# Two token pairs of 480 columns instead of one of 448, a shorter weight conversion and a bank for each of the last tiles, in an attention and two feed-forward layers on one core

## The chip, the core and the metric

The kernel runs on one core of a Trainium2 chip. The metric is the device time in microseconds (us); the time before is the median of three runs. Engines: TensorE (PE) with its weight loads (PEld), VectorE (DVE), ScalarE (ACT), GpSimd (POOL, unused here) and SyncE (SP), which issues nearly all DMAs.

## What is computed

```
# q, k, v: 1 x 6016 x 256;  w_in: 256 x 2048;  w_out: 2048 x 256, twice (float64)
qn = q / (norm(q, over tokens) + 1e-6);  kn the same
a = softmax(kn^T @ qn / tau)             # 256 x 256, over channels
x = v @ a                                # 6016 x 256
x = relu(x @ w_in)**2 @ w_out            # layer 1
h = x @ w_in2
out = maximum(0.01 * h, h) @ w_out2      # layer 2
```

## The kernel before

Tokens are columns: everything after the attention works on transposed activations, and a matmul streams one half of a token pair. Six pairs (`WIDTH`, line 59) cover the 6016 tokens, each of two halves of `WIDTH[p]` columns; `FIRST` holds where each begins. The program goes through the pairs twice, once for layer 1 and once for layer 2. In a pass over a pair the 2048 hidden channels are eight groups of 256; one group is a unit (`unit`, line 1396).

Values are float32 split in a high part, rounded by a copy to fp32r, and a low part, the difference (`low`, line 115). Each product is three matmuls (`mm3`, line 560): low by high, high by high, high by low. A unit has first products (x by `w_in`) and second products (g by `w_out`). Where the code says form P, the second products are eight of three matmuls; in form S they are seven, by Strassen's scheme, with sums kept in bank c (`yA`) and bank e (`yF`). First products are seven in every pair but the first of layer 1. `GROUPS` (line 56) says which groups of which pairs have form S: six of eight in the last two pairs of layer 1, seven in layer 2, five in its last pair. A unit with Strassen's first products and form P has 45 matmuls (21 and 24).

The weights come as float64 in pairs of 32-bit words. A `Unit` (lines 130 to 215) loads 256 x 256 of them into `wst`, makes float32 of them on DVE and ACT, rounds and splits them and stores them to DRAM for the passes that follow: `exponent`, `mantissa`, `mantissa_low`, `sign`, `high` on DVE and `rebias`, `round` on ACT. `w0` and `w1` are the low and the high word. The 16 units of layer 2, all but one in blocks with Strassen sums (`sums`, line 217), go through one buffer, `wis` (bufs=1): the cast in `round` fills it, DVE adds the low part, and SP stores it. The sums of layer 1's `w_out` (`wo_sums`, line 1307) use the same buffer.

The first two units of layer 1's `w_in` are converted during the attention (`converted`, line 307), step by step between the tiles of q and k. The scores are summed over 47 tiles on PE (line 404), the norms by squares on ACT and sums on DVE; then come the softmax and the fold of it into `w_in`. The first weights of `w_out` (`first_o`) begin there too.

At the end, the second half of the last pair takes its last two groups by tokens (`second_by_tokens`, line 596): g is the stationary side, and four tiles of 128 tokens by 256 channels come out, two to a bank. `finish_last` (line 612) adds to each the sums kept so far (`last_sums`) and stores it.

The order is not that of the code. `build` lists tasks with engine, cost, due time and the tasks they wait for; `simulate` (line 826) runs them by due time, in several turns (`TURNS`), with `PIPE` taken off the costs; the best plan is then written out engine by engine. `place` gives each result tile one of two rings, c or wst. On each engine instructions then run strictly in that order. `seeded` (line 978) says where a unit's first sum is made on PE and ACT rather than on DVE.

Of the kernel before, what the change touches and what calls it, by code (L numbers as in the profile page):

```python
# [19 lines left out]
P = 128  # L20

REBIAS = -896.0 * 2**23
# [7 lines left out]
def attn_moe_moe2(  # L33
# [25 lines left out]
    WIDTH = [512, 512, 512, 512, 448, 512]  # L59
# [32 lines left out]
    rebias = const.tile([P, 1], F32, name="rebias")  # L92
    nc.vector.memset(rebias, REBIAS)
# [36 lines left out]
    class Unit:  # L130
# [16 lines left out]
        def exponent(self):  # L147
            self.e = cpool.tile([P, 2, 2 * P], U32, tag="ce", name="ce")
            ts(self.e, self.w1, 0x7FF00000, None, op0=ALU.bitwise_and)

        def rebias(self):
            nc.scalar.activation(self.e, self.e, AF.Relu, bias=rebias, scale=8.0)

        def mantissa(self):
            self.m = cpool.tile([P, 2, 2 * P], U32, tag="cm", name="cm")
            ts(self.m, self.w1, 0x000FFFFF, 0x00100000, op0=ALU.bitwise_and, op1=ALU.bitwise_or)

        def mantissa_low(self):
            stt(raw(self.m), self.w0, 2.0**-32, self.m, op0=ALU.mult, op1=ALU.add)

        def sign(self):
            stt(self.e, self.w1, 0x80000000, self.e, op0=ALU.bitwise_and, op1=ALU.bitwise_or)

        def high(self):
            m, e = raw(self.m), raw(self.e)
            if self.blocks:
                self.x = cpool.tile([P, 8, P], F32, tag="whl", name="wr")
                if self.kind == "i":
                    to = self.x[:, :4].rearrange("p (k b) m -> p k (b m)", b=2)
                else:  # L170
                    to = self.x[:, :4].rearrange("p (k b) (q c) -> k p (b q) c", b=2, c=B)
                    m, e = (y.rearrange("p b (q k c) -> k p (b q) c", q=Q, k=KC) for y in (m, e))
                    for k in range(KC):
                        stt(to[k], m[k], 2.0**-20, e[k], op0=ALU.mult, op1=ALU.mult)
                    return
                stt(to, m, 2.0**-20, e, op0=ALU.mult, op1=ALU.mult)
                return
            stt(m, m, 2.0**-20, e, op0=ALU.mult, op1=ALU.mult)
            self.x = m
# [127 lines left out]
    def converted(units):  # L307

        units[0].exponent()
        later[ACT].append(units[0].rebias)  # L310
        yield
        for i, u in enumerate(units):
            if i + 1 < len(units):
                units[i + 1].exponent()
                later[ACT].append(units[i + 1].rebias)
                yield
            for step in (u.mantissa, u.mantissa_low, u.sign, u.high):
# [13 lines left out]
    with (  # L331
# [40 lines left out]
        STEPS = {2: 3, 3: 2}  # L372
# [80 lines left out]
        run(steps[1], 3)  # L453
# [29 lines left out]
        first_o.exponent()  # L483
# [112 lines left out]
    def second_by_tokens(n, fb):  # L596


        L, p, g = units[n]
        wo, gt = wo_t[L, p, g], g_t[n, 1]  # L600
        for t in range(WIDTH[p] // P):
            for m, (a, b) in enumerate(((0, 1), (0, 0), (1, 0))):
                nc.tensor.matmul(
                    y_bank(L, p, 1, t // 2)[:, t % 2 * C : (t % 2 + 1) * C],
                    gt[:, a, fb, t * P : (t + 1) * P],
                    wo[:, b, :, fb],
                    start=(g, fb) == (BY_TOKENS, 0) and m == 0 and t % 2 == 0,
                    stop=m == 2,
                    skip_group_check=True,
                )  # L610

    def finish_last():

        p = NP - 1
        ys = [y_t[2, p, 1, d] for d in range(KC)]
        to = rows(out, p, 1).rearrange("(t p) c -> p t c", p=P)
        o = [vpool.tile([P, 2, C], F32, tag="v", name="o"), tpool.tile([P, 2, C], F32, tag="s", name="o")]
        for b, copy in enumerate((nc.vector.tensor_copy, nc.scalar.copy)):
            ob = o[b].rearrange("p t (q k c) -> p t q k c", q=Q, k=KC)
            y = ys[b].rearrange("p (t k q c) -> p t q k c", t=2, q=Q, k=KC)  # L620
            if last_sums:
                sums = last_sums["t"].rearrange("p t (q k c) -> p t q k c", q=Q, k=KC)
                for t in range(2):
                    add(ob[:, t], y[:, t], sums[:, 2 * b + t])
            else:
                copy(ob, y)
# [136 lines left out]
    PIPE = {"DVE": (0.09, 0.45), "ACT": (0.1, 0.5), "PE": (0, 0.5), "POOL": (0, 0.6)}  # L763
# [5 lines left out]

    class Buf:  # L770


        def __init__(self, tag, bufs, due):
            self.due, self.bufs, self.users, self.alloc, self.tag = due, bufs, [], None, tag
            lines.setdefault(tag, []).append(self)
# [23 lines left out]
    def place(free_lines, held):  # L799

        known = {t: sorted((b.due, b.due + 60) for b in lines.get(t, ())) for t in free_lines}
        for b in sorted(lines.pop("any", ()), key=lambda b: b.due):

            def free(t):
                before = [e for d, e in known[t] if d <= b.due]
                return sorted(before)[-3] if len(before) >= 3 else 0

            b.tag = min(free_lines, key=free)
            known[b.tag].append((b.due, b.due + b.held))
# [78 lines left out]
    WHOLE = True  # L888
    TAIL = 12
    TURNS = 12  # L890
    FIRST_MIXED = min([p for L, p in GROUPS if L == 1], default=0)
    CONV_BEGIN, CONV_END = 1.2, 4.3
# [74 lines left out]
    BATCHES = {4: (4,), 5: (3, 2), 6: (3, 3), 7: (4, 3)}  # L967
# [23 lines left out]
    def build(base):  # L991
        tasks.clear()
        c_tag.clear()
        lines.clear()
        fixed, firsts, items = [], [], []
# [23 lines left out]
        ce_b = {0: Buf("ce", 2, -10)}  # L1019
# [3 lines left out]
        def convert(u, due, loaded=None, first=None, pace=4, begin=0):  # L1023
# [10 lines left out]
            if u is first_o:  # L1034
                ce = ce_b[0]
                t = None
            else:
                ce = Buf("ce", 2, d(0))
                t = T("DVE", 1.9, d(0), u.exponent, deps=deps, alloc=ce, uses=[w])
            re = T("ACT", 3.2, d(0.5), u.rebias, deps=[t], uses=[ce])  # L1040
            cm = Buf("cm", 2, d(1))
            t = T("DVE", 1.9, d(1), u.mantissa, deps=deps, alloc=cm, uses=[w])
            ml = T("DVE", 3, d(2), u.mantissa_low, deps=[t], uses=[w, cm])
            t = T("DVE", 3, d(3), u.sign, deps=[re, ml], uses=[w, ce])
            if blocks:
                raw_ = Buf("whl", 2, d(4))
                t = T("DVE", 3, d(4), u.high, deps=[t], alloc=raw_, uses=[ce, cm])
# [6 lines left out]
            else:  # L1054
                t = T("DVE", 3, d(4), u.high, deps=[t], uses=[ce, cm])
# [496 lines left out]
        def plain_items(n, order=order8):  # L1552
            L, p, g = units[n]
            if (L, p) == (2, NP - 1) and g >= BY_TOKENS:
                out_ = [plain_item(n, *o) for o in order[:4]]
                for fb in range(2):
                    x = queue(n, 6.35, second_by_tokens, (n, fb),
                              [low_of[n, 1], wo_ready[L, p, g], *y_after.get((L, p, 1, 0), ()), *y_after.get((L, p, 1, 1), ())],
# [157 lines left out]
        def combine_last(L, p):  # L1716
# [14 lines left out]
            y_after[L, p, 0, 1], y_after[L, p, 0, 0], y_after[L, p, 1, 1], y_after[L, p, 1, 0] = [y11], [y21], [y12], [y22]  # L1731
            key = L, p, "sums"
# [49 lines left out]
        free = simulate(PE(fixed, list(firsts), items))  # L1782
# [65 lines left out]
```

## Time and profile before

| | us |
|---|---|
| median of three runs | 1004.73 |
| lowest, highest | 1003.47, 1004.86 |
| the profiled execution's own time | 1005.9 |
| its span, first to last instruction | 1004.1 |
| PE busy | 998.2 |
| DVE busy | 920.8 |
| ACT busy | 803.7 |

The span is what the profile sees; 1.8 us lie around it. PE busy means that a matmul was under way, and matmuls overlap: the start of the next one is what counts, so the price of one is read from a row of the chain that merges several. Rows give their start, their length and, in brackets, how long the engine was idle before and what released it.

### The profile page before, as it was taken

Reading aid. Unit: us, or ns where it says so; the run is one execution under the profiler, and the core shown is the slowest. Engines: PE = TensorE matmul, PEld = TensorE weight load, DVE = VectorE, ACT = ScalarE, POOL = GpSimd, SP = SyncE. Lnnn points to the kernel's source line nnn. Section 1 sums busy time; section 2 is a strip of 40 time slices with the busy share of each in tenths; the row PEclk is TensorE's granted clock in tenths of the full one; section 3 lists DMA queues with packets and bytes.
Section 4 is the critical chain, followed back from the end, with each engine's and each line's share of the span. In section 5 each row is a group of like instructions: output and inputs, shape, how many; then the busy total and the mean of one; then the engine's idle time right before and its main releaser. Section 6 shows DMA issues by size and latency. Waiting matters only on the chain.

```text
span 1004.1 us, 13173 instructions
## 1 busy us (share of the span) xinstructions
PE 998.2 (99%) x4540; PEld 840.8 (84%) x4540; DVE 920.8 (92%) x1371; ACT 803.7 (80%) x1181; POOL 0.7 (0%) x6
## 2 busy tenths in 40 slices
PE   9999999999999999999999999999999999999998
PEld 8888888888887888898888888888888888998887
DVE  5999989999999999999998999999999999999985
ACT  6788877887878787887888888878888888887773
POOL 0000000000000000000000000000000000000000
PEclk9999999999999999999999999999999999999999
DMA  9796469869988977966756656577576577576643
GB/s 353 286 227 213 168 207 261 282 224 328 309 274 275 359 268 287 312 209 201 235 179 233 218 198 223 182 211 257 166 223 229 176 235 230 208 232 220 206 130 85
DMA packets 162035, 233.93 MB, mean 233 GB/s; under 512 B 53296, under 2 KB 97328, under 8 KB 159664
## 3 DMA queue, kind: packets, MB, share of 16 engines
q1 hardware_dynamic: 161248, 232.43, 70.6%
q8 instruction: 36, 0.59, 0.2%
q10 hardware_dynamic: 720, 0.66, 0.2%
q14 instruction: 31, 0.25, 0.1%
HBM read 186.12 MB, written 46.92 MB: 232 GB/s over the span
## 4 chain that ended last, share of the span: by engine, by line
PE 95%; DMA 3%; ACT 1%; DVE 1%; SPq 0%; issue 0%; ACTq 0%; DVEq 0%
PE y L562 36%; PE ha L562 20%; PE hb L562 15%; PE yA L562 7%; PE h L724 4%; PE yF L562 3%; PE hc L562 3%; PE sT L404 3%; PE he L562 2%; PE pw L265 1%; DMA qk<-in_k_dram 1%; DMA wo<-wis 1%; DMA qk<-in_q_dram 1%; DMA out_dram<-o 0%; ACT c L701 0%; ACT wis L205 0%
## 5 line engine op out<-in xcount | busy, mean ns | idle before, releaser
L562 PE MATMUL y<-g,wo 128*128 128x512 f32 (+1 forms) x1344 | 350.5, 387 | 0.0
L562 PEld LDWEIGHTS y<-g,wo 128*128 128x128 f32 x1344 | 252.2, 188 | 49.1
L562 PE MATMUL ha<-x,wi 128*128 128x512 f32 (+1 forms) x912 | 252.6, 385 | 0.2 <-ACT u L1421 0.2
L116 DVE TENSOR_TENSOR g<-c,g 128x1024 fp32r<-128x1024 f32 (+1 forms) x192 | 228.1, 1196 | 12.0 <-ACT g L694 7.0
L562 PEld LDWEIGHTS ha<-x,wi 128*128 128x128 f32 x912 | 170.9, 188 | 33.1 <-ACT c L1421 0.8
L562 PE MATMUL hb<-x,wi 128*128 128x512 f32 (+1 forms) x684 | 189.3, 385 | 0.0
L562 PEld LDWEIGHTS hb<-x,wi 128*128 128x128 f32 x684 | 128.0, 188 | 24.5 <-DVE c L571 0.6
L1526 DVE TENSOR_TENSOR c<-c 128x512 f32<-128x512 f32 (+1 forms) x208 | 139.9, 673 | 7.4
L1501 ACT CAST g<-c 128x1024 fp32r<-128x1024 f32 (+1 forms) x104 | 104.9, 1023 | 3.4 <-DVE c L1526 1.2
L116 DVE TENSOR_TENSOR b<-c,b 128x512 fp32r<-128x512 f32 (+1 forms) x156 | 102.9, 668 | 1.7 <-ACT b L1519 1.6
L1519 ACT CAST b<-c 128x512 fp32r<-128x512 f32 (+1 forms) x156 | 93.0, 608 | 13.0 <-DVE c L1526 7.1
L701 ACT ACTIVATE c<-c 128x1024 f32<-128x1024 f32 (+1 forms) x96 | 100.2, 1044 | 1.5
L694 ACT CAST g<-c 128x1024 fp32r<-128x1024 f32 (+1 forms) x88 | 91.9, 1046 | 2.0 <-PE y L562 0.3
L1421 ACT COPY w<-ha 128x512 f32<-128x512 f32 (+1 forms) x76 | 43.8, 576 | 51.2 <-PE ha L562 50.8
L711 ACT ACTIVATE c<-c 128x512 f32<-128x512 f32 (+1 forms) x98 | 60.7, 621 | 7.7 <-DVE c L571 7.5
L1421 ACT COPY u<-ha 128x512 f32<-128x512 f32 (+1 forms) x76 | 43.7, 575 | 7.3 <-PE ha L562 5.3
L724 PE MATMUL h<-x,wi 128*128 128x512 f32 x192 | 47.9, 391 | 0.0
L116 DVE TENSOR_TENSOR x<-xr,x 128x1024 fp32r<-128x1024 f32 (+3 forms) x44 | 46.6, 1064 | 0.1
L562 PE MATMUL y<-b,ws 128*128 128x512 f32 (+1 forms) x156 | 43.0, 384 | 0.0
L562 PE MATMUL yA<-g,wo 128*128 128x512 f32 (+1 forms) x156 | 43.0, 384 | 0.0
L562 PE MATMUL y<-b,wo 128*128 128x512 f32 (+1 forms) x156 | 43.0, 384 | 0.0
L562 PE MATMUL yF<-g,ws 128*128 128x512 f32 (+1 forms) x156 | 43.0, 383 | 0.0
(133 smaller groups left out, 1269.9 us busy)
## 6 DMA issues: line engine op xcount, KB each, us to landing
wi<-wi SPq DMA_DIRECT2D x80, 896.0 KB, 5.7
wo<-wo SPq DMA_DIRECT2D x84, 512.0 KB, 4.7
ws<-wo SPq DMA_DIRECT2D x120, 128.0 KB, 3.4
wi<-wi SPq DMA_DIRECT2D x24, 512.0 KB, 5.0
wst<-in_moe_w_in_dram SPq DMA_DIRECT2D x16, 512.0 KB, 6.1
wst<-in_moe_w_out_dram SPq DMA_DIRECT2D x16, 512.0 KB, 5.8
wi<-wis SPq DMA_DIRECT2D x8, 896.0 KB, 4.9
wo<-wis SPq DMA_DIRECT2D x7, 1024.0 KB, 5.9
```

Of the source, the lines that this page charges most:

```text
L116: tt(lo, x, raw(hi), op=ALU.subtract)
L265: nc.tensor.matmul(pw[:, i * 2 * P : (i + 1) * 2 * P], eT[:, a, j, i * P : (i + 1) * P], whl[g][:, b, j], start=t == 0 and (i == 0 or g == 0),
L404: nc.tensor.matmul(sT[j][:, :C], t[:, 0, i, j * P : (j + 1) * P], t[:, 1, i], start=n == 0 and i == 0, stop=last_tile and i == g - 1,)
L562: nc.tensor.matmul(ps, a[m], b[n], start=first and i == 0, stop=i == 2, skip_group_check=True)
L694: nc.scalar.copy(g_t[n, half][:, 0, :, :w], c)
L701: nc.scalar.activation(c, c, AF.Square)
L711: nc.scalar.activation(c, c, AF.Prelu, alpha=0.01)
L724: nc.tensor.matmul(h_t[n, half, fb][:, :w], a[i], b[j], start=start, stop=stop, skip_group_check=True)
L1421: nc.scalar.copy(to, h(0))
L1501: nc.scalar.copy(g_t[n, name][:, 0, :, :w], result(n, half, w))
L1519: nc.scalar.copy(b_t[n, name][:, 0, :w], c(half, fb))
L1526: tt(c(*to), c(*a), c(*b), op=ALU.subtract)
```

## The change

`WIDTH` becomes 512, 512, 480, 480, 512, 512; the sum is the same. By `seeded`, the first two units of a layer-2 pair that is wider than the one before start without a seed: that was the sixth pair and is the fifth.

The conversion reads the high word as a float32, multiplies it by 2 to the -112 on ACT (`scaled`), which moves the exponent from the float64 offset, shifts the result left by three bits (`shifted`), puts the sign back with an AND and an OR (`sign`, as before but into the same tile), and ORs in the top three bits of the low word (`high`). The low word is cut there, where before it was added as a number. `exponent`, `rebias`, `mantissa` and `mantissa_low` go, and the tile `ce` with them (its ring stays for `ws`).

Each of the four last token tiles has a bank of its own: two of the y banks, c and e. The matmuls now also wait for the last reader of c and e.

The planner gets other numbers: `PIPE` 0.18 for DVE and 0.22 for ACT (0.09 and 0.1) and 0.6 for PE's latency (0.5), `TURNS` 14 (12), `CONV_END` 3.8 (4.3). `place` sorts no more and takes a `held` time if there is one; `HOLD` is False. `STEPS` for the first converted unit is one step after tile 2 and three after tile 3 (three and two). `BATCHES` gets two entries that no pair uses.

```diff
-    WIDTH = [512, 512, 512, 512, 448, 512]
+    WIDTH = [512, 512, 480, 480, 512, 512]
...
-        def exponent(self):
-            self.e = cpool.tile([P, 2, 2 * P], U32, tag="ce", name="ce")
-            ts(self.e, self.w1, 0x7FF00000, None, op0=ALU.bitwise_and)
-        def rebias(self):
-            nc.scalar.activation(self.e, self.e, AF.Relu, bias=rebias, scale=8.0)
-        def mantissa(self):
+        def scaled(self):
             self.m = cpool.tile([P, 2, 2 * P], U32, tag="cm", name="cm")
-            ts(self.m, self.w1, 0x000FFFFF, 0x00100000, op0=ALU.bitwise_and, op1=ALU.bitwise_or)
-        def mantissa_low(self):
-            stt(raw(self.m), self.w0, 2.0**-32, self.m, op0=ALU.mult, op1=ALU.add)
+            nc.scalar.activation(raw(self.m), raw(self.w1), AF.Copy, scale=2.0**-112)
+        def shifted(self):
+            ts(self.m, self.m, 3, None, op0=ALU.logical_shift_left)
         def sign(self):
-            stt(self.e, self.w1, 0x80000000, self.e, op0=ALU.bitwise_and, op1=ALU.bitwise_or)
+            stt(self.m, self.w1, 0x80000000, self.m, op0=ALU.bitwise_and, op1=ALU.bitwise_or)
         def high(self):
...
-            stt(m, m, 2.0**-20, e, op0=ALU.mult, op1=ALU.mult)
-            self.x = m
+            def last(to, m, w0):
+                stt(to.bitcast(U32), w0, 29, m, op0=ALU.logical_shift_right, op1=ALU.bitwise_or)
...
         for t in range(WIDTH[p] // P):
+            if first:
+                by_token.append(y_bank(L, p, 1, t) if t < KC else bank("ce"[t - KC], "y"))
             for m, (a, b) in enumerate(((0, 1), (0, 0), (1, 0))):
                 nc.tensor.matmul(
-                    y_bank(L, p, 1, t // 2)[:, t % 2 * C : (t % 2 + 1) * C],
+                    by_token[t][:, :C],
...
-                    start=(g, fb) == (BY_TOKENS, 0) and m == 0 and t % 2 == 0,
+                    start=first and m == 0,
...
+        for t, y in enumerate(by_token):
+            y = y[:, :C].rearrange("p (k q c) -> p q k c", q=Q, k=KC)
+            add(o[t // 2][:, t % 2].rearrange("p (q k c) -> p q k c", q=Q, k=KC), y, sums[:, t])
         nc.sync.dma_start(to[:, :2], o[0])
-        nc.scalar.dma_start(to[:, 3:], o[1][:, 1:])
-        nc.sync.dma_start(to[:, 2:3], o[1][:, :1])
+        nc.scalar.dma_start(to[:, 2:3], o[1][:, :1])
+        nc.sync.dma_start(to[:, 3:], o[1][:, 1:])
```

DVE in the attention, where the second unit is converted between the sums of squares and the norms. Before (the page's line numbers; `wst` is the loaded weights, `ce` and `cm` the exponent and the mantissa, `small` the norms):

```order
L449 RECIPROCAL rtau<-tau_sb 128x1
L149 TENSOR_SCALAR ce<-wst 128x512
L156 TENSOR_SCALAR cm<-wst 128x512
L159 SCALAR_TENSOR_TENSOR cm<-wst,cm 128x512
L162 SCALAR_TENSOR_TENSOR ce<-wst,ce 128x512
L458 RECIPROCAL small<-small 128x4
```

DVE at the same place now (lines of the changed file):

```order
L431 RECIPROCAL rtau<-tau_sb 128x1
L146 TENSOR_SCALAR cm<-cm 128x512
L149 SCALAR_TENSOR_TENSOR cm<-wst,cm 128x512
L440 RECIPROCAL small<-small 128x4
L441 TENSOR_SCALAR small<-small 128x4
```

Two of the four steps ahead of the norms are gone; the shift reads what ACT has scaled.

PE at the very end, with buffer numbers: `y_8849` and `y_8805` are the two banks of the last token tiles before.

```order
L562 MATMUL y_8798<-g_9289,wo_9119 128x512 x6
L562 MATMUL y_8829<-g_9289,wo_9119 128x512 x6
L603 MATMUL y_8849<-wo_9015,g_9230 128x256 x6
L603 MATMUL y_8805<-wo_9015,g_9230 128x256 x6
L603 MATMUL y_8849<-wo_9015,g_9230 128x256 x6
```

PE at the same place now; the four y names from `y_8765` on are four banks.

```order
L543 MATMUL y_8716<-g_9191,wo_9048 128x512 x6
L543 MATMUL y_8758<-g_9191,wo_9048 128x512 x6
L587 MATMUL y_8765<-wo_8933,g_9144 128x256 x3
L587 MATMUL y_8724<-wo_8933,g_9144 128x256 x3
L587 MATMUL y_9225<-wo_8933,g_9144 128x256 x3
L587 MATMUL y_9229<-wo_8933,g_9144 128x256 x3
```

Each tile's three matmuls now fill a bank that holds nothing else; the order of the tiles is the same.

ACT in the third pair of layer 1, around a cast into `wis` (`ha` and `hc` are banks of first products, `c` results, `g` their rounded copies). Before:

```order
L1421 COPY u<-ha 128x512
L205 CAST wis<-wr 128x1024
L1421 COPY w<-ha 128x512
L1436 ACTIVATE c<-ha 128x512
L701 ACTIVATE c<-c 128x1024
L694 CAST g<-c 128x1024
```

ACT at the corresponding place now:

```order
L1403 COPY u<-ha 128x480
L1403 COPY w<-ha 128x480
L192 CAST wis<-wr 128x1024
L1418 ACTIVATE c<-ha 128x480
L681 ACTIVATE c<-c 128x2x480
L674 CAST g<-c 128x2x480
```

The cast stands one copy later in its unit; what is behind it waits with it when its buffer is still being stored.

## Rows read from the trace of the kernel before

**Rows 1.** The page: busy time and share by engine; PE's granted clock in 40 slices.

```profile
PE 998.2 (99%) x4540; PEld 840.8 (84%) x4540; DVE 920.8 (92%) x1371; ACT 803.7 (80%) x1181; POOL 0.7 (0%) x6
PEclk9999999999999999999999999999999999999999
```

**Rows 2.** The chain that ended last: start us, us, engine, names, line, matmuls.

```profile
67.84 1.43 PE pw L265 x12
...
402.04 1.40 PE y L562 x6
...
420.30 1.24 PE y L562 x6
...
464.00 1.21 PE y L562 x6
...
641.28 1.36 PE y L562 x6
```

**Rows 3.** Groups by line and form, matmuls of 448 columns: count, busy us, mean ns.

```profile
L562 PE MATMUL ha<-x,wi 128*128 128x448 f32 x192 | 49.7, 367 | 0.0
...
L562 PE MATMUL yA<-b,ws 128*128 128x448 f32 x39 | 9.9, 366 | 0.0
```

**Rows 4.** Waits of PE's weight loads: us in total, times, longest us.

```profile
PEld ha L562 <- ACT c L1421: 0.8, 2, 0.4
PEld ha L562 <- ACT u L1421: 0.6, 1, 0.6
PEld hb L562 <- DVE c L571: 0.6, 2, 0.4
...
PEld hb L562 <- DVE c L569: 0.5, 2, 0.4
```

**Rows 5.** Groups by line and form, three steps of the conversion.

```profile
L152 ACT ACTIVATE ce<-ce,rebias 128x512 uint32<-128x512 uint32 x32 | 23.0, 723 | 3.1 <-DVE ce L149 3.1
L159 DVE SCALAR_TENSOR_TENSOR cm<-wst,cm 128x512 f32<-128x512 uint32 x32 | 22.1, 689 | 0.5
...
L149 DVE TENSOR_SCALAR ce<-wst 128x512 uint32<-128x512 uint32 x32 | 13.5, 421 | 1.6 <-DMA wst<-in_moe_w_in_dram 1.3
```

**Rows 6.** Stretch of a layer-2 pair: us, busy PE, PEld, DVE, ACT, POOL, clock, DMA.

```profile
772.00:848.00 76.00, 76.00 (x337) 63.04 (x336) 72.05 (x99) 63.30 (x100) 0.00 (x0) 1.00 0.66 212
```

**Rows 7.** Timeline of the last ten us: start us, us, engine, line, what.

```profile
994.29 5.91 PE L603 MATMUL y<-wo,g 128*128 128x256 f32 x48
...
999.52 1.47 DVE L571 TENSOR_TENSOR o<-y,sums 128x256 f32<-128x256 f32 x4 [3.72 <-DMA out_dram<-o]
...
1001.02 0.35 ACTq L628 DMA_DIRECT2D out_dram<-o  x1
```

**Rows 8.** Timeline in the attention, the second unit's conversion and the first maximum.

```profile
44.32 0.68 DVE L162 SCALAR_TENSOR_TENSOR ce<-wst,ce 128x512 uint32<-128x512 uint32 x1
...
45.40 0.27 ACT L455 ACTIVATE small<-pn,small 128x4 f32<-128x4 f32 x1 [1.29 <-PE pn L378]
...
47.69 0.60 PE L477 MATMUL s<-ident,sTs 128*128 128x128 f32 x4
47.86 0.42 DVE L149 TENSOR_SCALAR ce<-wst 128x512 uint32<-128x512 uint32 x1
...
48.21 0.42 DVE L489 TENSOR_REDUCE mx<-s 128x1 f32<-128x256 f32 x1
```

**Rows 9.** A cast into wis, PE near it (timeline), and the tile wis by itself.

```profile
302.94 0.84 PE L562 MATMUL hb<-x,wi 128*128 128x512 f32 x3
...
303.55 1.05 ACT L205 CAST wis<-wr 128x1024 fp32r<-128x1024 f32 x1 [1.03 <-DMA wo<-wis]
...
307.66 0.96 PE L562 MATMUL ha<-x,wi 128*128 128x512 f32 x3 [0.17 <-ACT u L1421]
...
L116 DVE TENSOR_TENSOR wis<-wr,wis x21: 1216/1219/1227, 180.2 to 404.8; 128x1024 fp32r<-128x1024 f32 x21
...
DMA to landing us min/median/max: 3.8/5.2/9.3
```

More of the change, by code (lines that the diff above doesn't have):

```diff
@@ L20 @@
 P = 128
-REBIAS = -896.0 * 2**23
 def raw(ap):
@@ L178, in high @@
-            stt(m, m, 2.0**-20, e, op0=ALU.mult, op1=ALU.mult)
-            self.x = m
+            def last(to, m, w0):
+                stt(to.bitcast(U32), w0, 29, m, op0=ALU.logical_shift_right, op1=ALU.bitwise_or)
+            self.x = raw(self.m)
+            if not self.blocks:
+                last(self.x, self.m, self.w0)
+                return
+            self.x = cpool.tile([P, 8, P], F32, tag="whl", name="wr")
+            if self.kind == "i":
+                last(self.x[:, :4].rearrange("p (k b) m -> p k (b m)", b=2), self.m, self.w0)
+                return
@@ L181, in into @@
+            to = self.x[:, :4].rearrange("p (k b) (q c) -> k p (b q) c", b=2, c=B)
+            m, w0 = (y.rearrange("p b (q k c) -> k p (b q) c", q=Q, k=KC) for y in (self.m, self.w0))
+            for k in range(KC):
+                last(to[k], m[k], w0[k])
         def into(self):
@@ L307, in converted @@
     def converted(units):
[L309 to L317, printed above, removed]
+        for u in units:
+            later[ACT].append(u.scaled)
+            yield
+            for step in (u.shifted, u.sign, u.high):
                 step()
@@ L452, in attn_moe_moe2 @@
         flush(ACT)
-        run(steps[1], 3)
+        run(steps[1], 2)
         y, m, z, r = (small[:, i] for i in range(4))
@@ L799, in place, with times @@
     def place(free_lines, held):
-        known = {t: sorted((b.due, b.due + 60) for b in lines.get(t, ())) for t in free_lines}
+        def times(b):
+            return held_then[b.nr] if held_then else (b.due, b.due + getattr(b, "held", 60))
+        known = {t: [times(b) for b in lines.get(t, ())] for t in free_lines}
         for b in sorted(lines.pop("any", ()), key=lambda b: b.due):
+            mine = times(b)
             def free(t):
-                before = [e for d, e in known[t] if d <= b.due]
-                return sorted(before)[-3] if len(before) >= 3 else 0
+                before = sorted(e for d, e in known[t] if d <= mine[0])
+                return before[-3] if len(before) >= 3 else 0
             b.tag = min(free_lines, key=free)
-            known[b.tag].append((b.due, b.due + b.held))
+            known[b.tag].append(mine)
             lines.setdefault(b.tag, []).append(b)
@@ L1033, in convert @@
                 w, deps = loaded, ()
[L1034 to L1044, printed above, removed]
+            cm = Buf("cm", 2, d(0))
+            t = T("ACT", 3.2, d(0), u.scaled, deps=deps, alloc=cm, uses=[w])
+            t = T("DVE", 1.9, d(1), u.shifted, deps=[t], uses=[cm])
+            t = T("DVE", 3, d(2), u.sign, deps=[t], uses=[w, cm])
             if blocks:
                 raw_ = Buf("whl", 2, d(4))
-                t = T("DVE", 3, d(4), u.high, deps=[t], alloc=raw_, uses=[ce, cm])
+                t = T("DVE", 3, d(4), u.high, deps=[t], alloc=raw_, uses=[w, cm])
                 for i in range(4):
@@ L1782, in build @@
         free = simulate(PE(fixed, list(firsts), items))
+        if HOLD:
+            held_then[:] = [(b.alloc.start, max(x.end for x in b.users)) if b.alloc else (b.due, b.due + 60) for b in buffers]
         first_start = {x.n: x.start for x in tasks if x.engine == "PE" and getattr(x, "name", "") == "F1"}
```

49 lines of the change are left out of this document (16 added, 33 removed).

## The prediction

> **What bounds the kernel now.** I read the page's busy table first: TensorE (PE) is busy for 998.2 of 1004.1 us and its granted clock is full in all 40 slices [rows 1]. A busy share that near to one leaves two ways to a shorter time: less matmul time, or a shorter head and tail. So the next view is the chain of work that ended last. Almost all its rows are matmul groups, and their lengths give the price of one matmul at each width [rows 2]: six of 512 columns take 1.36 us (226.7 ns each), twelve of 256 take 1.43 us (119 ns each), six of 448 take 1.24 us in one stretch (206.7 ns) and 1.21 us in another (201.7 ns). The clock granted there is the upper of the two levels, 2.4 GHz, where a column takes 0.417 ns; 512 columns are 213.3 ns, so a matmul of 512 pays 13.3 ns on top, one of 256 pays 12.5 ns, but one of 448 pays 15 to 20 ns. The reader is to see that the narrow pair is dearer per column than the others. 681 matmuls have 448 columns; the listing by form holds them (first and a last group in [rows 3]; there are eight groups). Then I read who made PE wait: the weight loads' four largest waits in the matmul stages sum to 2.5 us [rows 4]. VectorE (DVE) is busy for 72.05 of 76 us, 95%, in a late stage [rows 6], so it is close behind, but it does not set the end.
>
> **The change part by part.**
>
> *Widths.* The number of matmuls stays, but columns move. With 480, 480, 512 in place of 512, 512, 448, the two 480 pairs hold 2 x 360 matmuls in layer 1 (8 groups of 21 first and 24 second products) and 2 x 339 in layer 2, 1398 in all; the 681 of 448 are gone, and 717 fewer have 512. Before: 717 x 226.7 ns = 162.5 us, and 681 at the middle of their two rates, 204.2 ns, = 139.1 us; together 301.6 us. After: 1398 times the price of a 480, which no row shows. At the 13.3 ns on top that 512 and, nearly, 256 pay it is 200 + 13.3 = 213.3 ns and 298.2 us, a gain of 3.4 us. At the 20 ns that 448 pays at worst it is 220 ns and 307.6 us, a loss of 6.0 us. On the straight line between 448 and 512 it is 215.5 ns and 301.2 us, a gain of 0.4 us. I take 213.3 ns: two of the three widths pay that surcharge, and 448 itself comes within 2 ns of it in one of its stretches. It is the weakest number here, and both ends go into the range. All of it lies on the path, since PE has no idle time to hide it in. Matmuls of 512 that alternate with 448 are slower too (six in 1.40 us [rows 2]); that is 0.04 us a group and stays out of the sum.
>
> The Trainium skill, "TensorE: Matmul & The Clock Gate", section "Back-to-back issue gap", makes a warm matmul's gap its columns at 2.4 GHz plus a fixed 2.5 ns, 215.8 ns at 512. The trace has 226.7 ns there, so the constant is larger here, and 448 does not fit any constant; by such a rule only the columns saved would count, which is the third rival below.
>
> *Conversion of weights.* For each of 32 units DVE loses the exponent mask (421 ns) and the low mantissa (689 ns); the mantissa mask, the same form as the exponent's, becomes a shift, and the sign and the last step stay two-operand steps [rows 5]. That is 1.11 x 32 = 35.5 us less DVE work. ScalarE (ACT) exchanges one 723 ns activation for another of the same size; the nearest plain copies of 512 elements take less, so it gains or loses nothing that matters. None of this is on PE's path: what PE can get back is the waits that end at DVE or ACT, 2.5 us at the very most, and a new order can add others. I take 0 for it, with -2.5 to +3 for the range. The cover is PE's own queue of second products; where that runs out, DVE's work shows.
>
> *Head.* The second unit is converted beside the norms. Its exponent, masks and sum end on DVE by 45.0 us, before the root that ACT starts at 45.40 us [rows 8], so removing them frees nothing. The first output unit's exponent at 47.86 us stands ahead of the first row maximum (48.21 us), but the scores it reads come from transposes that start at 47.69 us and take 0.60 us [rows 8]; less than 0.1 us can come of it. The first unit's scaling now waits on ACT for its load, where the exponent waited on DVE; the squares behind it wait for later loads of q and k. I take 0.
>
> *Tail.* Four adds of 0.37 us run from 999.52 to 1000.99 us, the last two of them after the last matmul's end at 1000.20 us, because the two tiles in the second bank are released together [rows 7]. With a bank each, the third add can start when its own tile is done and only one stays behind the end; the last store then leaves SP's queue instead of ACT's. That is 0.4 us less, wholly on the path. The four banks are two that the pair's own products have left and the two of the shared sums, whose last readers are now waited for; they ran long before.
>
> *Planner.* New costs reorder DVE and ACT, conversions end half a pair earlier, and the two units per layer-2 pair that start unseeded move from the sixth pair to the fifth. None has a price by itself; they are in the -2.5 to +3.
>
> Sum: -3.4 - 0.4 = -3.8 us. Against the profiled execution's own 1005.9 us (span 1004.1 us and 1.8 us around it) that is 1002.1 us; that execution lies 1.2 us above the median of the runs, 1004.73 us, so the forecast is **1000.9 us**.
>
> **The rivals.**
>
> 1. *A 480 pays part of 448's surcharge* (the straight line): -0.4 - 0.4 gives 1003.9 us. For it: only full and half banks are seen at 13 ns. Against: 480 is no nearer to 448 than to 512.
> 2. *A 480 pays 448's worst surcharge*, and twice as many matmuls pay it: +6.0 - 0.4 gives 1010.3 us. It decides for slower from 216.0 ns a matmul on (1398 x 216.0 = 302.0, the 301.6 and the tail's 0.4). For it: 448 held 206.7 ns for long, so it is no accident of one place.
> 3. *Columns plus a constant.* If the surcharge were the same at each width, only the columns saved would count: six groups of the mixed pairs do 21 instead of 24 products, so 6 x 3 x 64 = 1152 columns, 0.5 us; with the tail 1003.8 us. The 448 rows speak against it.
> 4. *The single buffer of converted blocks becomes a wait.* One cast into wis stands in ACT's order about once per unit. A round through the buffer takes 1.05 us cast, 1.22 us low part and a store of 5.2 us (median; 9.3 us longest) [rows 9], 7.5 to 11.6 us. A unit at 480 columns lasts 45 x 0.2133 = 9.6 us, where at 512 it lasted 10.2. Once in the kernel before ACT stood still for 1.03 us for such a store, and groups of PE just behind it took 0.96 instead of 0.84 us [rows 9]. From a landing of 7.3 us on it decides; if half the 16 units of the two 480 pairs in layer 1 pay 1.0 us, it is +8 us: 1008.9 us. Against: the median landing leaves 2 us.
> 5. *The lighter DVE also removes the waits*: a further -2.5 us, 998.4 us.
>
> That the change does not do what it says can be left out for the adds and the widths; for the lighter conversion it is the forecast itself, that it brings nothing.
>
> **How the numbers follow.** Forecast 0.45; rival 1 0.20; rival 2 0.12; rival 3 0.05; rival 4 0.10; rival 5 0.08. About 0.2%, 2 us, is what a measurement of this kernel tells from no change: faster means below 1002.7 us, slower above 1006.7 us. Faster: nine tenths of the forecast (its -2.5 to +3 reaches over the bound), a quarter of rival 1, all of rival 5: 0.54. Slower: rivals 2 and 4: 0.22. The rest, 0.24, is the same. The range runs from 998.0 us (rival 5 and a little) to 1008.5 us; it leaves out rival 2 and half of rival 4. The forecast's own range is 998.4 to 1003.9 us.
>
> **What would show it.** In the chain, six matmuls of 480 columns take 1.28 us if the forecast holds, 1.29 to 1.30 by rival 1, 1.32 by rival 2, steadily over whole pairs. The page has no exponent rows and about 35 us less DVE time. In the tail one add lies behind the last matmul. The weight loads' waits on ACT and DVE stay near 2.5 us; a wait of ACT's cast into wis on its store, more than once, would be rival 4. The forecast is wrong if 480 is not a cheap width, or if those waits grow past 3 us.

## The result

The changed kernel takes 1010.57 us (median of six runs, 1009.67 to 1011.40) where the kernel before, beside it, took 1004.80 us: 1.0056 of its time, 95% interval 1.0043 to 1.0069. It is slower by 5.8 us. The forecast was 1000.9 us with a range of 998.0 to 1008.5 us: wrong in sign, and outside the range.

The profiled execution after took 1011.4 us, its span 1009.5 us (before: 1005.9 and 1004.1 us). The page's busy table and granted clock, against [rows 1]:

```profile
PE 1002.1 (99%) x4540; PEld 838.9 (83%) x4540; DVE 893.4 (88%) x1306; ACT 802.2 (79%) x1181; POOL 0.7 (0%) x6
PEclk9999999999999999999999999999999999999999
```

The clock is full throughout, PE is busy for 3.9 us longer, and DVE for 27.4 us less. The chain of work around a 480 pair, against [rows 2] (start us, us, engine, names, line, matmuls):

```profile
297.52 1.30 PE y L543 x6
298.82 0.65 PE hc L543 x3
```

Six matmuls of 480 columns take 1.30 us, 216.7 ns each; 213.3 was forecast. The waits of PE's weight loads in the matmul stages (us in total, times, longest), against [rows 4]:

```profile
PEld ha L543 <- ACT c L1403: 1.7, 5, 0.5
PEld hc L543 <- ACT w L1403: 1.6, 1, 1.6
...
PEld hc L543 <- ACT c L1403: 1.1, 3, 0.4
PEld hb L543 <- DVE c L552: 1.0, 4, 0.4
...
PEld y L543 <- DMA ws<-wo: 0.6, 1, 0.6
PEld hb L543 <- DVE c L550: 0.5, 2, 0.3
```

These six are 6.5 us, where the four of before were 2.5 us, and most of them end at a copy by ACT (L1403).

**The account.** To add up the whole span, I took from the trace the time from each matmul's start to the next one's, from the first feed-forward matmul on, and compared it with the price of its width when nothing waits (226.67, 216.67, 202.67 and 120 ns for 512, 480, 448 and 256 columns; the first experiment measures them). What is over by more than 30 ns is a wait of PE; matmuls that run at a lower clock behind a long wait are counted there too. Before: prices 943.2 us, waits 2.0 us in 16 places. After: prices 945.6 us, waits 4.9 us in 34. The difference of the spans, 5.4 us, is then 2.4 us of prices, 2.9 us of waits and 0.65 us of a later first feed-forward matmul (52.85 instead of 52.20 us), less 0.5 us of small steps under 30 ns. In the other traces that matmul starts anywhere from 51.75 to 52.73 us, and in g2 below, whose engines run the changed kernel's order, at 52.39 us, so I take the 0.65 us as a difference between executions. The price and the waits are what is to be explained.

Two of the waits, as the trace shows them. The longest is at 258 us; the chain there reads (start us, us, what):

```profile
249.01 9.47 DMA wo<-wis
...
258.51 1.05 ACT wis L192
259.56 0.46 ACT w L1403
...
260.06 0.92 PE hc L543 x3
```

A store from the single buffer wis lands 9.47 us after its issue. ACT's next cast into wis (L192) stands still for it, the copy behind that cast frees PE's bank late, and PE loses 1.3 us. This is the fourth rival's mechanism, once. The usual wait is smaller and comes in pairs. PE's timeline in the second token pair (start us, us, engine, line, what, matmuls):

```profile
160.34 0.84 PE L543 MATMUL ha<-x,wi 128*128 128x512 f32 x3
161.01 0.84 PE L543 MATMUL hb<-x,wi 128*128 128x512 f32 x3
161.69 0.84 PE L543 MATMUL y<-g,wo 128*128 128x512 f32 x3
162.49 0.96 PE L543 MATMUL ha<-x,wi 128*128 128x512 f32 x3
```

and ACT's beside it:

```profile
160.90 1.05 ACT L674 CAST g<-c 128x1024 fp32r<-128x1024 f32 x1
161.85 0.58 ACT L1403 COPY c<-ha 128x512 f32<-128x512 f32 x1
```

PE comes back to the bank ha after six other matmuls. ACT copies that bank only behind a long cast, until 162.43 us, and PE starts 0.11 us late; the matmul after it is late by another 0.11 us (the group takes 0.96 instead of 0.84 us), since its weight load, too, started late. So this short wait of PE costs 0.11 us more than itself; the account counts the two as two waits.

### The profile page after: what moved, and what is told of

It reads as the page before. It is cut to its first block, busy times and chain, and to the rows that moved or that the text cites. A ratio compares the mean times of both kernels' runs of the same rounds, so it can differ in the third digit from the quotient of the medians.

```text
span 1009.5 us, 13175 instructions
## 1 busy us (share of the span) xinstructions
PE 1002.1 (99%) x4540; PEld 838.9 (83%) x4540; DVE 893.4 (88%) x1306; ACT 802.2 (79%) x1181; POOL 0.7 (0%) x6
## 4 chain that ended last, share of the span: by engine, by line
PE 93%; DMA 4%; ACT 1%; DVE 1%; issue 0%; SPq 0%; ACTq 0%
PE y L543 35%; PE ha L543 20%; PE hb L543 15%; PE yA L543 7%; PE h L704 4%; PE yF L543 3%; PE hc L543 3%; PE sT L386 3%; PE he L543 2%; DMA qk<-in_k_dram 2%; PE pw L252 1%; DMA wo<-wis 1%; DMA xr<-x 1%; DMA ws<-wo 1%; ACT c L681 0%
## 5 line engine op out<-in xcount | busy, mean ns | idle before, releaser
L1403 ACT COPY w<-ha 128x512 f32<-128x512 f32 (+1 forms) x76 | 43.9, 578 | 46.7 <-PE ha L543 46.4
L691 ACT ACTIVATE c<-c 128x512 f32<-128x512 f32 (+1 forms) x98 | 61.0, 623 | 13.3 <-DVE c L552 12.6
L1403 ACT COPY u<-ha 128x512 f32<-128x512 f32 (+1 forms) x76 | 43.8, 576 | 5.2 <-PE ha L543 2.0
```

Of the source, the lines that this page charges most:

```text
L691: nc.scalar.activation(c, c, AF.Prelu, alpha=0.01)
L1403: nc.scalar.copy(to, h(0))
```

## The experiments

The change has three parts: the widths (W), the new conversion with the last tiles' banks (C), and the planner's numbers (N: what it takes off each instruction of DVE and ACT and adds on the way to the next engine, and where the conversions end). W and N re-make the whole order, and so does C through its costs. The runs with the new C also have the changed `place` and `STEPS`, those with the old C do not. So the runs are read by their median against the kernel before in the same comparison, and by the sum of PE's waits in their trace.

| run | W | C | N | median us | ratio, 95% | span us | PE's waits us |
|---|---|---|---|---|---|---|---|
| before | old | old | old | 1004.8 | | 1004.1 | 2.0 |
| f1_conv_banks | old | new | old | 1006.5 | 1.0010 to 1.0032 | 1004.8 | 3.5 |
| e1_widths | new | old | old | 1015.7 | 1.0086 to 1.0114 | 1015.1 | 12.0 |
| f4_newplan | old | old | new | 1015.3 | 1.0091 to 1.0118 | 1013.2 | 11.2 |
| e3_oldplan | new | new | old | 1006.8 | 1.0002 to 1.0020 | 1003.9 | 0.8 |
| e2_oldwidths | old | new | new | 1010.6 | 1.0038 to 1.0063 | 1009.1 | 6.9 |
| g1_widths_plan | new | old | new | 1008.7 | 1.0025 to 1.0053 | 1007.8 | 3.6 |
| changed | new | new | new | 1010.6 | 1.0043 to 1.0069 | 1009.5 | 4.9 |

A trace shows one execution and the median many; e3 and h2 (below) were profiled in executions near their lowest time.

### The price of a width

Nothing but matmuls (24 groups of three for each width, weights changing at each), with no waits; the rest of the kernel is left out.

> Leaves out the whole computation: after one load it streams only matmuls, 24 groups of three (as the kernel's own) at each of ten widths from 512 to 256 columns, then 8 groups of 512 alternating with 480 and 8 with 448; the output is zeros. It measures the price of a matmul by width with DVE, ACT and DMA at rest. Theory S (the surcharge belongs to the width itself): 512 takes 226.7 ns, 480 takes 216 to 217, 448 takes 202 to 207, so 72 of 480 take 15.6 us. Rival (it comes from the traffic around PE in the kernel): 480 takes 213.3 ns, 72 of them 15.36 us, and 448 takes 200.0 ns, 14.4 us.

The windows, one for each width from its first start to the next width's (stretch, us, PE busy, matmuls touched, clock, DMA share, GB/s); each holds 72 matmuls, of 512, 496, 480, 464, 448, 432, 416, 384, 320 and 256 columns:

```profile
23.54:39.86 16.32, 16.32 (x74) 1.00 0.10 34
39.86:55.70 15.84, 15.84 (x74) 1.00 0.01 1
55.70:71.30 15.60, 15.60 (x74) 1.00 0.00 0
71.30:86.42 15.12, 15.12 (x74) 1.00 0.00 1
86.42:101.01 14.59, 14.59 (x73) 1.00 0.00 0
101.01:115.11 14.10, 14.10 (x74) 1.00 0.01 1
115.11:128.55 13.44, 13.44 (x74) 1.00 0.00 0
128.55:141.04 12.49, 12.49 (x74) 1.00 0.00 1
141.04:151.59 10.55, 10.55 (x74) 1.00 0.01 2
151.59:160.22 8.63, 8.63 (x74) 1.00 0.00 0
```

Divided by 72: 226.7, 220.0, 216.7, 210.0, 202.6, 195.8, 186.7, 173.5, 146.5, 119.9 ns. Over the columns at 2.4 GHz that is 13.3 ns at 512, 496, 416, 384, 320 and 256, but 16.7 at 480 and 464 and 16 at 448 and 432. A 480 is one of the dear widths. In the stream the gaps of the 480s alternate: half of them are 212 or 213 ns, the forecast's price, and half are 220 or 221 ns, while those of the 512s are 226 or 227 ns; what makes the difference is not shown. In the stream's last part, where groups of three alternate, a 512 takes 236 ns between 480s and 232 ns between 448s; where that happens in the kernel, the account has it among the small steps. With no wait anywhere the new widths cost 1398 x 216.7 + 2766 x 226.7 = 929.9 us, the old ones 681 x 202.7 + 3483 x 226.7 = 927.5 us: they lose 2.4 us.

### Widths alone

```diff
# the kernel before
-    WIDTH = [512, 512, 512, 512, 448, 512]
+    WIDTH = [512, 512, 480, 480, 512, 512]
```

> The kernel before with the new widths alone. Theory S: 1398 matmuls at 216.7 ns and 717 fewer of 512 against 681 of 448 at 202 to 207 cost about 2 us, so 1006.8 us, up to 1.5 us either way for the plan that is made anew. Rival W (the waits of the changed plan are the cause, not the width): within 0.7 us of the kernel before.

1015.7 us, 10 us above the kernel before. The 480s run at the same 216.7 ns; 12.0 us of waits make the rest, 2.6 us of them matmuls at a lower clock behind the longest. The longest, in PE's timeline:

```profile
416.63 0.84 PE L562 MATMUL y<-b,wo 128*128 128x512 f32 x3
421.00 1.65 PE L562 MATMUL hb<-x,wi 128*128 128x512 f32 x3 [3.53 <-DVE c L569]
```

and what DVE did before that L569:

```profile
414.68 2.14 DVE L1526 TENSOR_TENSOR c<-c 128x512 f32<-128x512 f32 x3
...
419.70 0.65 DVE L116 TENSOR_TENSOR b<-c,b 128x512 fp32r<-128x512 f32 x1
420.27 0.68 DVE L569 CUSTOM_DVE_ANT_0 c<-w,hb 128x512 f32<-128x512 f32 x1
```

DVE is busy for all of the 4 us that PE stands (the window at the end of the document): the step that frees PE's bank simply stands behind eight others from 414.68 us on, the last part of a converted block among them. No instruction became dearer; the order came out so. What such a wait does to the clock stands at the end.

### Old widths, and old planner's numbers, under the rest of the change

```diff
# e2_oldwidths: the changed kernel
-    WIDTH = [512, 512, 480, 480, 512, 512]
+    WIDTH = [512, 512, 512, 512, 448, 512]
# e3_oldplan: the changed kernel
-    PIPE = {"DVE": (0.18, 0.45), "ACT": (0.22, 0.5), "PE": (0, 0.6), "POOL": (0, 0.6)}
+    PIPE = {"DVE": (0.09, 0.45), "ACT": (0.1, 0.5), "PE": (0, 0.5), "POOL": (0, 0.6)}
-    TURNS = 14
+    TURNS = 12
-    CONV_BEGIN, CONV_END = 1.2, 3.8
+    CONV_BEGIN, CONV_END = 1.2, 4.3
```

> The changed kernel with the old widths, 512 x 4, 448, 512; the conversion, the last tiles' banks and the planner's numbers stay changed. Theory S alone: about 2 us under the changed kernel, 1008.6 us, the waits of the plan staying. If the plan's waits hang on the widths too, 1004.0 to 1005 us. Rival W: no change from the changed kernel, 1010 to 1011 us.

> The changed kernel with the planner's old numbers: PIPE, TURNS and CONV_END, so that conversions spread over half a pair more. Theory S: the price of 480 stays; at most the 1.3 us wait behind the store of wis goes: 1009.0 to 1010.6 us. Rival W (the denser conversions and the waits that they bring are the cause): 1005 to 1007 us.

The old widths win nothing back (1010.6 us): their order has 6.9 us of waits, 2 us more than the changed kernel's, and that eats the 2.4 us. The planner's old numbers win 3.8 us back (1006.8 us); the waits fall from 4.9 to 0.8 us. The place shown above, in e3's trace:

```profile
160.29 2.88 PE L543 MATMUL y<-g,wo 128*128 128x512 f32 x12
163.01 0.84 PE L543 MATMUL ha<-x,wi 128*128 128x512 f32 x3
```

Twelve second products stand in a row here, and ACT has 2.7 us for what it owes PE before ha comes again; in the changed kernel they stand three by three between first products. TURNS plays no part: with 12 in place of 14, the changed kernel's order on every engine is word for word the same, and so it is for f1 and f4.

### Which of the planner's numbers, and the parts alone

f1_conv_banks is the changed kernel with both edits above (C alone). f2_pipe has the first line of e3's edit only, f3_convend the last only. f4_newplan is e3's edit the other way about in the kernel before.

> The changed kernel with the old widths and the planner's old numbers (margins of the engines, end of the conversions): the new conversion and the last tiles' banks alone. Theory A (the time is the sum of the matmuls' prices by width and of PE's waits in the plan; conversion and banks cost nothing themselves): against the run with the old planner's numbers the width price falls from 1398 x 216.7 + 2766 x 226.7 = 929.9 us to 681 x 202.7 + 3483 x 226.7 = 927.5 us, so 1006.8 - 2.4 = 1004.4 us if its waits of PE stay near 0.8 us, and later by what they are longer; the same as before within its noise, or 0.1% under it. Theory B (the new conversion itself costs, being split between ScalarE and VectorE): 1006.5 us or more, with waits on ACT's scaled copy.

> The changed kernel with the planner's old margins for the engines' instructions alone (0.09, 0.1, 0 us taken off and 0.45, 0.5, 0.5 us to the next engine); conversions still end at 3.8 pairs. Theory A1 (the margins made the waits): PE's waits fall from 4.9 us to under 2 us and the pairs of 0.11 us behind ACT's copies in the second to fourth pair of the first layer go; 1007 us. Theory A2 (the earlier end of the conversions made them): waits near 5 us, 1010.6 us.

> The changed kernel with the conversions spread to 4.3 pairs as before and the new margins. Theory A1 (the margins made the waits): still 4 to 6 us of waits on PE, pairs of 0.11 us behind ACT's copies among them; 1010 us. Theory A2 (the earlier end of the conversions): under 2 us of waits; 1007 us. If both give about 1009 us, neither number alone is the cause and the plan's waits hang on their meeting.

> The kernel before with the planner's three new numbers alone: old widths, old conversion, old banks. Theory A1 (the plan made under the new margins waits, whatever is converted how): the pairs of 0.11 us behind ACT's copies show up here too, 3 to 6 us of waits, 1007 to 1010 us. Rival (the new numbers suit any conversion, and the waits come of the new conversion's load on ACT): waits near the 2.0 us of before, 1005 us.

f2 took 1009.4 us (1.0034 to 1.0058) with 4.3 us of waits, f3 1009.1 us (1.0034 to 1.0057) with 6.0 us. By the medians each alone gives back about a third of the 3.8 us that both do; these intervals overlap that of the changed kernel, so the third is not sure, but neither number is the cause by itself. What does go with the margins is the pairs of 0.11 us at 145, 162 and 172 us: they are in the changed kernel, e2, f3, f4 and g1 (below), and in none of before, e1, e3, f1 and f2. C alone takes 1006.5 us, 2 us above the 1004.4 us that theory A gives for short waits; but the waits are 3.5 us, 2.7 us more than e3's, and none of them is at the scaled copy, where theory B put them (DVE stood for that copy once, 1.3 us, and PE did not). A second kind of wait, at 697 us in f1:

```profile
696.82 1.23 DVE L1228 TENSOR_TENSOR xr<-xr 128x1024 f32<-128x1024 f32 x1 [3.17 <-DMA xr<-x]
...
697.96 0.68 DVE L552 TENSOR_TENSOR c<-w,hb 128x512 f32<-128x512 f32 x1
...
698.70 0.96 PE L543 MATMUL hb<-x,wi 128*128 128x512 f32 x3 [0.79 <-DVE c L552]
```

DVE stands 3.17 us at a sum of xr for its load, and the step that PE needs (L552) stands behind it. f4 shows that the new numbers do nothing good for the old conversion: 1015.3 us, with 11.2 us of waits, 3.45 us of them at 339 us, where ACT's cast into wis waited 4.1 us for a store.

### The last corner, the store's queue and the planned landing

```diff
# g2_pool: the changed kernel
-                nc.sync.dma_start(wo_d[self.L, self.g], raw(self.to))
+                nc.gpsimd.dma_start(wo_d[self.L, self.g], raw(self.to))
# g3_f1_lands26: f1; g4_after_lands26: the changed kernel
-    LANDS = 14
+    LANDS = 26
```

g1_widths_plan is the kernel before with W and N.

> The kernel before with the new widths and the planner's new numbers, but the old conversion and the old last banks: the last corner of the eight. Theory A (every re-made plan has waits of its own, which do not add up from one plan to the next, and the lighter conversion takes a part of them away): 1012 to 1018 us, above the changed kernel by what the lighter conversion saves. Rival (widths and numbers each cost their own 10 us): 1004.8 + 10.3 + 10.6 = 1025.7 us.

> The changed kernel with the stores of the split w_out blocks issued by GpSimd instead of SyncE; the order on TensorE, ScalarE and VectorE is word for word that of the changed kernel. Theory (the 1.31 us wait of PE at 258 us is ACT's cast into wis waiting for such a store, issued 9.5 us before its landing among SP's other transfers): if the store lands sooner from a queue of its own, that wait and the 0.11 us behind it go: 1010.6 - 1.4 = 1009.2 us. If its landing is set by the traffic of the 16 engines, it stays: 1010.6 us.

> The kernel with the new conversion, the new last banks, old widths and the planner's old numbers (its waits: 3.5 us, of which 2.0 us at two places where VectorE waits for the load of xr), planned with 26 instead of 14 units (5.9 instead of 3.2 us) from a transfer's issue to its landing, as its traces have 5.1 to 9.1 us for xr. Theory (the plan puts work behind loads that land later than it thinks): waits fall to about 1 us, 1006.5 - 2.5 = 1004.0 us, a little under before. Rival (a re-made plan's waits are as good as drawn by lot): anywhere between 1004 and 1012 us.

> The changed kernel planned with 26 instead of 14 units to a transfer's landing. Theory (late landings): of its 4.9 us of waits the 1.4 us behind the store of wis and the 0.5 us behind the load of ws go, the pairs of 0.11 us behind ACT's copies stay: 1008.7 us. Rival (by lot): 1006 to 1014 us.

W and N together (g1) cost 3.8 us where each alone cost over 10 us. That settles that the parts have no prices that add up. The run lies under the changed kernel too, against my expectation that the lighter conversion helps there.

g2 keeps the order of PE, ACT and DVE and moves the stores to GpSimd's queue. The store was issued 2 us sooner (246.98 us), yet it landed only 1.1 us sooner, 10.4 us after its issue instead of 9.5 us; ACT's cast still waited for it, and PE lost 0.68 instead of 1.31 us there. The waits of PE's weight loads and of ACT at that place:

```profile
PEld hc L543 <- ACT w L1403: 0.9, 1, 0.9
ACT wis L192 <- DMA wo<-wis: 0.9, 1, 0.9
```

Another wait of 1.07 us came up at 284 us. The median went from 1010.6 to 1010.2 us, which the executions do not tell apart. A queue of its own does not make the store land in time; by the account the fourth rival's wait is 1.4 us (1.31 and the 0.11 behind it) of the 5.4 us between the spans.

The two runs with later planned landings do not bear out the idea that the plan's landings (14 units, about 3.2 us, a unit being near one 512-column matmul) are the cause, although loads of xr really land 5.1 to 9.1 us after their issue: g3 took 1021.1 and g4 1024.4 us, with 16.9 and 18.6 us of waits, each with one wait of about 10 us near 425 us, in which PE waits for a step of DVE. Planned with truer landings the order came out worse; since the whole order is re-made here too, this does not clear the landings of every part in the waits.

### One number in small steps

f1's kernel (C alone) with the conversions to end at 4.25, 4.35, 4.4 and 4.5 pairs instead of 4.3, the changed kernel with 3.85 instead of 3.8, and the new widths under the best of them (i1).

> New conversion and last banks, old widths, old margins, conversions to end at 4.25 instead of 4.3 pairs. Theory (lot): the waits of TensorE are drawn anew, anywhere from 0.8 to 12 us, and the time is 927.5 us of matmuls by width, those waits, and 74 us of head and tail plus 1.8 us outside the span: 1004 to 1015 us. Rival (smooth): within 0.5 us of the 3.5 us of waits at 4.3, 1006.5 us. Under both no pairs of 0.11 us behind ACT's copies at 145, 162 and 172 us, as in all five orders with the old margins.

> As the last, with 4.35 pairs. Theory (lot): 1004 to 1015 us, with no regard to the run at 4.25. Rival (smooth): 1006 to 1007 us, on the other side of 1006.5 than 4.25.

> As the last, with 4.4 pairs. Theory (lot): 1004 to 1015 us. Rival (smooth): a line through 4.25, 4.3 and 4.35 gives it within 0.5 us.

> The changed kernel with conversions to end at 3.85 instead of 3.8 pairs. Theory (lot): its long waits (1.31 us at 258 us, 0.4 us at 734 us) come at other places and of other lengths, 1008 to 1016 us; the pairs of 0.11 us behind ACT's copies at 145, 162 and 172 us stay, for they go with the new margins. Rival (smooth): 1010.6 us with the same long waits.

> The order that ran fastest so far (new conversion and last banks, old margins, conversions to end at 4.4 pairs), with the new widths instead of the old. Theory (480 columns cost 216.7 ns each): 1003.9 + 2.4 = 1006.3 us and as much more as its waits exceed 1.0 us. The forecast's own price (213.3 ns): 1003.9 - 2.3 = 1001.6 us at the same waits.

> Old widths, new conversion and last banks, old margins, conversions to end at 4.5 pairs. If the trend goes on (waits of 3.8, 3.5, 2.2 and 1.0 us at 4.25, 4.3, 4.35 and 4.4): under 1 us of waits, 1003.5 us. If not, a long wait at a new place: 1005 us or more.

| run | end | median us (lowest, highest) | ratio, 95% | PE's waits us |
|---|---|---|---|---|
| h1_end425 | 4.25 | 1006.5 (1004.5, 1009.8) | 1.0007 to 1.0027 | 3.8 |
| f1_conv_banks | 4.3 | 1006.5 (1004.8, 1009.8) | 1.0010 to 1.0032 | 3.5 |
| h2_end435 | 4.35 | 1007.1 (1004.8, 1009.2) | 1.0010 to 1.0032 | 2.2 |
| h3_end440 | 4.4 | 1003.9 (1003.4, 1004.8) | 0.9982 to 0.9999 | 1.0 |
| i2_end450 | 4.5 | 1005.0 (1004.2, 1006.5) | 0.9992 to 1.0010 | 2.1 |
| h4_after_end385 | 3.85 | 1010.8 (1010.2, 1011.0) | 1.0042 to 1.0070 | 5.4 |
| i1_480_end440 | 4.4, new W | 1007.7 (1006.4, 1008.4) | 1.0017 to 1.0038 | 3.2 |

My theory of a lot drawn at every step falls: at 4.25 to 4.35 the same waits stand at the same places (446 and 610 us in all three, 545 and 697 us in two), and the changed kernel's 1.3 us at 258 us is there at 3.85 as at 3.8. The smooth rival does not hold for larger steps: at 4.4 those waits are gone, and at 4.5 there are others. These orders kept their waits until a step was large enough to move the instructions that made them.

The kernel with 4.4 is the only one under the kernel before: by 1.0 us, 0.1%. Its interval reaches up to 0.9999 and it is the best of eighteen changed kernels, so it may be no gain at all. All the idle time there that a load of xr ended, from the view of that tile (us, times):

```profile
  DMA xr<-x: 1.6, 3
...
DMA to landing us min/median/max: 4.9/7.3/8.2
```

and in f1, with loads that land no later:

```profile
  DMA xr<-x: 7.6, 4
...
DMA to landing us min/median/max: 5.1/7.1/9.1
```

The executions of f1, h1 and h2 spread over 4.4 to 5.3 us, those of h3 over 1.4 us; that the first three hang on when xr lands in each execution fits this, but was only argued. i1 is h3 with the new widths: 3.7 us slower by the median and 4.0 us by the span: 2.4 us of prices and 2.2 us of longer waits, less 0.6 us of small differences. The forecast's 480 would have made it 2.3 us faster.

**All runs together.** Span less prices less waits is 57.3 to 59.3 us in all 19 traces of whole kernels, before and after among them, while the spans go from 1002.4 to 1023.1 us. So the time of this kernel is the prices of its widths, PE's waits, and a head and tail that hardly change.

## Why the prediction was wrong

**What bounds the kernel**: right. PE's matmuls are the time, and everything else counts only through PE's waits.

**Widths: the term that failed first, -3.4 us.** The step was "I take 213.3 ns: two of the three widths pay that surcharge". The price was 216.7 ns, above the 216.0 ns that the second rival named as the point from which it decides. Against the 301.6 us of before in the forecast, 1398 x 216.7 = 302.9 us is +1.3 us; against the clean price of 448, +2.4 us. The rows could not tell 480's price, and that was said; 512 and 448 are equally far from 480, and the mistake was to let it follow 512 and 256 on a count of two against one. The stream has both groups, and 480 is with 448. Rival 1's row (1.29 to 1.30 us for six) is what the trace shows, but rival 1 put 215.5 ns on it. Rival 2's 1010.3 us is near the measured 1010.57 us by luck: it has 6.0 us of price and no new wait, where the runs have 2.4 us of price and 2.9 us of waits. The prediction also says that both ends of the price go into the range; they do not, for the range stops at 1008.5 us.

The Trainium skill, "TensorE: Matmul & The Clock Gate", section "Back-to-back issue gap", has columns at 2.4 GHz plus 2.5 ns for a warm matmul. The stream has 13.3 to 16.7 ns on top, and no single constant. So the third rival fails too.

**Conversion and planner: 0, with -2.5 to +3: the term that was mis-sized.** DVE lost what was forecast; its steps after, against [rows 5]:

```profile
L149 DVE SCALAR_TENSOR_TENSOR cm<-wst,cm 128x512 uint32<-128x512 uint32 x32 | 22.1, 691 | 1.0
L143 ACT ACTIVATE cm<-wst 128x512 f32<-128x512 f32 x32 | 21.3, 673 | 2.4 <-DVE wr L153 1.2 <-DVE wo L110 1.0
L146 DVE TENSOR_SCALAR cm<-cm 128x512 uint32<-128x512 uint32 x32 | 13.4, 420 | 0.3 <-ACT cm L143 0.2
```

One step of 689 ns and one of 421 ns per unit are gone, and busy DVE time fell by 27.4 us, less than the 35.5 us of steps: its records, which overlap, fell by 33.0 us in sum. PE got nothing of it, as said. The step that failed here was "I take 0 for it": the waits grew by 2.9 us, at the end of the range given. Of these 2.9 us, 1.4 are the wait for wis with its 0.11 us behind it, the rest the pairs behind ACT's copies and two at 470 and 734 us. "None has a price by itself" was literally so, and still the planner's numbers were the largest single thing to undo: 3.8 us. In the seven other orders of the eight corners and in f2 and f3 the waits lie between 0.8 and 12.0 us, and in g3 and g4 they are 16.9 and 18.6 us, so +3 was too low by several times as a bound for an edit that re-makes this kernel's order.

**Rival 4** was the mechanism of the longest wait, and the words "more than once" were its test: ACT's casts stood for stores of wis three times, 3.6 us in all, but PE felt one of them, 1.3 us, not eight; near the other two it lost 0.05 us at most. In the kernel before, too, there was a second such stand that the prediction did not count, 0.5 us behind a store of layer 1's sums.

**Tail: right in kind.** The timeline, against [rows 7]:

```profile
999.75 5.91 PE L587 MATMUL y<-wo,g 128*128 128x256 f32 x48
...
1004.62 1.50 DVE L552 TENSOR_TENSOR o<-y,sums 128x256 f32<-128x256 f32 x4 [3.36 <-DMA out_dram<-o]
...
1006.15 0.36 SPq L609 DMA_DIRECT2D out_dram<-o  x1
```

The matmuls end at 1005.66 us and one add, the last, begins after that. From the last matmul's start to the end of the span it is 4.15 us here against 4.19 us before; over the traces with the new banks it is mostly 3.93 us (ten of fifteen, highest 4.39), with the old ones 4.19 to 4.49 us. So it wins about 0.26 us, not 0.4, as far as traces of whole kernels tell; banks alone were not run.

**Head: 0, and 0.65 us was seen**, which I put down to the execution, as g2 with the same order has 0.19 us.

**Late stage.** DVE's 72.05 of 76 us [rows 6] became:

```profile
772.00:848.00 76.00, 76.00 (x351) 65.21 (x350) 72.54 (x105) 61.15 (x101) 0.00 (x0) 1.00 0.64 216
```

PE is busy for all of it, before and after. DVE is no lighter there: the steps of the conversion end by 405 us in both kernels, so their relief does not reach this stage.

What stays open: why the waits fall where they do in one order and not in another. Which instruction is late can be read in each trace; which number of the planner would avoid it, these runs do not tell. Whether the kernel before with its own conversion would also gain from an end at 4.4 pairs was not tried.

## What to carry to other kernels

Where a planner sets the order, do not price an edit by what it removes: the re-made order brings waits of its own, and their size (here 0.8 to 18.6 us in a kernel of 1005) belongs in the error bar of the forecast, on both sides of zero. Look in the trace for the steps that PE needs and that stand behind a long step or a transfer on an in-order engine. And before widths are exchanged, measure the price of each width in a stream of nothing else; here the price of 480 did not lie where its neighbours would put it by a line or by a constant.

## What the runs showed of the chip

**The price of a width is not columns plus a constant.** 13.3 ns on top of the columns at 512, 496, 416, 384, 320 and 256 columns, 16 to 16.7 ns at 480, 464, 448 and 432.

**A long wait of PE costs again afterwards.** In e1, around the wait of 3.69 us (stretch, us, busy PE, PEld, DVE, ACT, POOL, clock, DMA share, GB/s):

```profile
417.00:421.00 4.00, 0.47 (x3) 0.05 (x1) 4.00 (x7) 4.00 (x6) 0.00 (x0) 0.87 0.53 178
421.00:427.00 6.00, 6.00 (x15) 4.70 (x16) 3.34 (x5) 2.99 (x5) 0.00 (x0) 0.52 0.62 219
427.00:440.00 13.00, 13.00 (x59) 10.76 (x58) 12.20 (x18) 10.36 (x15) 0.00 (x0) 1.00 0.50 164
```

The granted clock is 0.52 in the 6 us behind it, close to the lower level of 1.2 GHz, and a 512 takes 0.2 us longer there, thirteen times: 2.6 us on top of the wait. PE had stood for 3.7 us before. f4's wait of 3.45 us was followed by a clock of 0.61 over 4.4 us. Behind the wait of 1.3 us in the changed kernel, the clock stayed full:

```profile
258.70:260.00 1.30, 0.21 (x1) 0.00 (x0) 0.00 (x0) 1.30 (x3) 0.00 (x0) 1.00 1.18 240
260.00:266.00 6.00, 5.94 (x27) 5.18 (x28) 5.71 (x11) 5.82 (x9) 0.00 (x0) 1.00 0.85 262
```

**A wait can cost 0.11 us more than it lasts.** The weight load, too, starts late, and the group of three at 162.49 us takes 0.96 instead of 0.84 us. In the account of the changed kernel thirteen waits, the one of 1.31 us among them, have a second of 0.10 to 0.12 us right behind; eight have none.
